# A fused retention and mixture-of-experts kernel: when weight chunks are loaded, when an early group is routed, and which banks the experts write to

## The chip, the cores and the metric

The kernel runs on one core of one Trainium2 chip. The metric is the device time of one execution in microseconds (us). TensorE is PE (matmuls) and PEld (its weight loads) in the rows, VectorE is DVE, ScalarE is ACT, GpSimd is POOL, and SP is the engine whose queue issues the plain DMAs.

## The reference

Eight batches of eight heads, 576 positions of 64 numbers each, go through a masked product without a softmax. The result is 4608 tokens of 512 numbers. Each token is sent to the one of eight experts whose embedding it is most like, and the expert's two-layer network is applied to it.

```python
scores = q @ k.T / sqrt(64)
x = (scores * gamma[h] ** (i - j) * (i >= j)) @ v          # per batch and head
x = x.transpose(0, 2, 1, 3).reshape(4608, 512)
logits = normalized(x) @ normalized(expert_emb).T / tau
e = argmax(logits); gate = softmax(logits)[e]
out = gate * (relu(x @ w1[e]) @ w2[e])                     # 512 -> 1024 -> 512, float32
```

## The kernel before

**The stream.** The 4608 tokens are 36 tiles of 128, and two batches are nine tiles, so the jobs around a tile repeat every nine tiles. Within this part (`manual_schedule`) every engine does its work in the order in which the code emits it. Iteration t of the loop does the following.

- It issues the loads of q/k and k/v of tile t+6 (`load_qk`, `load_kv`, seven buffers each).
- It emits the scores of the next tile, `emit_A(t + 1)`, into the two banks `pa`, and `emit_mask(t + 1)`, two VectorE products (L600) that read these banks. So the scores of tile t+2 cannot start before the mask of t+1 has read the banks.
- GpSimd scales the values of tile t+2 (`scale_v`, L583).
- `emit_QT`, `emit_O` and `emit_U` make the output of tile t in the two banks `po` and add to the running state in `pst`; `emit_X` (VectorE) takes the output from `po`.
- `emit_T(t - 1)` turns the previous tile by four matmuls against the identity (L134); ScalarE copies it (L689), SP stores it to `xd`.
- The jobs in the list `jobs[t]` come last: the steps of the routing, and the split of a weight chunk.

**Routing.** The tiles are eight groups of four or five. A group whose last tile is tl gets `route_logits` in iteration tl+1, `route_turn` and `route_head` in tl+2, `route_rank` and `route_onehot` in tl+3 (some ten VectorE steps, the last of them L308 to L323), `route_table` in tl+4. Group 6 (tiles 27 to 30) is the last that is routed inside the stream. Behind its table, in iteration 34, come `slots_to_tokens` and the first three gathers (`gather(0, i)`, an indirect DMA issued by GpSimd, L375), which fetch expert 0's first 384 tokens from `xd`. Behind the loop, `xprep(0, i)` turns what was gathered (L134, then L397 and L398), and the first layer of expert 0 starts.

**Weights.** Each weight matrix comes in four chunks of 128 x 1024 numbers. A chunk is loaded to a `raw` buffer (of seven), copied to a rounded part by ScalarE (L188), and VectorE makes the remainder (L189). Chunks of the first matrix are loaded and split in the jobs of iterations 12, 16, 20 and 24:

```python
wq = wsplit_tasks(0)
for i in range(4):
    at(12 + 4 * i, wq.pop(0))
```

**Experts.** This part is ordered by a planner, which moves instructions on each engine by its own estimates. For an expert e, `mm1` or `mm1_round` make the first layer, by 12 matmuls for each of eight blocks f and two token ranges, into the banks `pm` (range 0) and `pa`, `pst` (range 1), evicted by L805 and L806. `mm2(e, i)` makes the second layer for the i-th 128 tokens by 24 matmuls (L866); ScalarE multiplies by the gate (L873) and GpSimd scatters the rows (L874). `mm2` writes to two banks in turn, which are the halves of the stream's one tile `po`, except for i = 2, which has a `pm` bank:

```python
po = psp.tile([P, 2, 512], F32, name="po")
pso = Banks([po[:, 0, :], po[:, 1, :]])
```

The tokens of expert e+1 are gathered meanwhile (`gather`), turned by a transposing DMA (`xturn`, L413 and L414) and joined again (`xjoin`, L420, L397, L398).

Of the kernel before, what the change touches and what calls it, by code (L numbers as in the profile page):

```python
# [9 lines left out]
F32 = mybir.dt.float32  # L10
# [8 lines left out]
P = 128  # L19
B, H, S, D = 8, 8, 576, 64  # L20
# [8 lines left out]
NT = N // P  # L29
# [7 lines left out]
RW = 1032  # L37
# [56 lines left out]
def retention_moe(ctx: ExitStack, tc: tile.TileContext, qk, kv, embT, tau, w1, w2, cst, out):  # L94
# [6 lines left out]
    my = ctx.enter_context(tc.tile_pool(name="my", bufs=3))  # L101
    psp = ctx.enter_context(tc.tile_pool(name="psp", bufs=1, space=PSUM))
    pa = [psp.tile([P, 512], F32, name=f"pa{i}") for i in range(2)]
    po = psp.tile([P, 2, 512], F32, name="po")
    pst = psp.tile([P, 512], F32, name="pst")

    class Banks:
# [6 lines left out]
            return self.banks[(self.n - 1) % len(self.banks)]  # L114

    psa = Banks(pa + [pst])
    pso = Banks([po[:, 0, :], po[:, 1, :]])
    psm = Banks([psp.tile([P, 512], F32, name=f"pm{i}") for i in range(3)])

    def after(*ins):  # L120
# [48 lines left out]
    ss_all = keep.tile([P, NT], F32, name="ss_all")  # L169


    def wsplit_tasks(n):

        e, second = divmod(n, 2)
        src = (w2 if second else w1)[e]

        def step(c):
            raw = rawp.tile([P, RW], F32, name="raw")[:, :1024]
            if second:
                nc.sync.dma_start(  # L180
                    out=raw.rearrange("p (c n) -> p c n", c=2),
                    in_=src[c * 256 : (c + 1) * 256, :].rearrange("(c p) n -> p c n", p=P),
                )
            else:
                nc.sync.dma_start(out=raw, in_=src[c * P : (c + 1) * P, :])
            sl = wslot[n % 3]
            hi = sl[:, 0, c * 1024 : (c + 1) * 1024]
            nc.scalar.copy(hi, raw)  # L188
            nc.vector.tensor_tensor(  # L189
                out=sl[:, 1, c * 1024 : (c + 1) * 1024], in0=raw, in1=hi.bitcast(F32), op=ALU.subtract  # L190
            )

        return [lambda c=c: step(c) for c in range(4)]


    grp = {}
# [1 line left out]
    def group_tiles(b):  # L198
        t0 = (b // 2) * 9 + (0 if b % 2 == 0 else 4)
        return t0, (4 if b % 2 == 0 else 5)  # L200
# [170 lines left out]
    def gather(e, i, rows=N):  # L371
        a = _slot(e, i)
        t = rawp.tile([P, RW], F32, name="raw")
        xg[e, i] = t
        return nc.gpsimd.indirect_dma_start(  # L375
            out=t[:, :DM],
            out_offset=None,
            in_=xd[:rows, :],
            in_offset=bass.IndirectOffsetOnAxis(ap=gid[:, a : a + 1], axis=0),
        )  # L380
# [96 lines left out]
    with ExitStack() as att:  # L477
# [4 lines left out]
        a2 = att.enter_context(tc.tile_pool(name="a2", bufs=2))  # L482
        a1 = att.enter_context(tc.tile_pool(name="a1", bufs=1))

        qkt, kvt = {}, {}

        def load_qk(t):
# [241 lines left out]
        jobs = {}  # L729

        def at(t, f):
            jobs.setdefault(t, []).append(f)
# [4 lines left out]
        for b in range(B - 1):  # L737
            t0, G = group_tiles(b)
            tl = t0 + G - 1
            at(tl + 1, lambda b=b: route_logits(b))  # L740
            at(tl + 2, lambda b=b: (route_turn(b), route_head(b)))
            at(tl + 3, lambda b=b: (route_rank(b), route_onehot(b)))
            at(tl + 4, lambda b=b: route_table(b))
            if b == B - 2:
                at(tl + 4, lambda: slots_to_tokens(0, 3))
                for i in range(3):
                    at(tl + 4, lambda i=i: gather(0, i, group_tiles(B - 1)[0] * P))
                at(tl + 4, route_bump)
        wq = wsplit_tasks(0)
        for i in range(4):  # L750
            at(12 + 4 * i, wq.pop(0))

        emit_A(0)
        emit_mask(0)
        scale_v(0, nc.vector)
# [2 lines left out]
        for t in range(NT):  # L758
            if t + NLOAD - 1 < NT:
                load_qk(t + NLOAD - 1)  # L760
                load_kv(t + NLOAD - 1)
            if t + 1 < NT:
                emit_A(t + 1)
                emit_mask(t + 1)
            if t + 1 < KT:
                decay(t + 1)
            if t + 2 < NT:
                scale_v(t + 2, nc.gpsimd)
            if t % KT == 4:
                emit_O(t)  # L770
                emit_QT(t)
                emit_U(t)
            else:
                emit_QT(t)
                emit_O(t)
                emit_U(t)
            emit_X(t)
            if t > 0:
                emit_T(t - 1)
            for f in jobs.pop(t, ()):  # L780
                f()
        assert not jobs, jobs
        b = B - 1
# [9 lines left out]


    with ExitStack() as moe:
        mw = moe.enter_context(tc.tile_pool(name="mw", bufs=1, reuse_waits="tile"))
        hs = mw.tile([P, 2, NF, CAP], F32R, name="hs")
        late["xs1"] = mw.tile([P, 2, NP, C1], F32R, name="xs1")
# [166 lines left out]
    with tc.If(ntile > 0):  # L965
        with ExitStack() as ov:
# [57 lines left out]
            with tc.For_i(0, ntile, 1) as i:  # L1024
                ex = nc.sync.value_load(tei[0:1, bass.ds(i, 1)], min_val=0, max_val=NE - 1)
                w1s = op.tile([P, NP, FF], F32, name="w1s")
                nc.sync.dma_start(out=w1s, in_=w1[bass.ds(ex, 1)].rearrange("o (d p) n -> p (o d) n", p=P))
                w2s = op.tile([P, NF, DM], F32, name="w2s")
                nc.sync.dma_start(out=w2s, in_=w2[bass.ds(ex, 1)].rearrange("o (f p) n -> p (o f) n", p=P))
                ent = op.tile([P, 1], F32, name="ent")  # L1030
                nc.sync.dma_start(out=ent, in_=od[bass.ds(i * P, P), :])
                of = op.tile([P, 3], F32, name="of")
                nc.vector.tensor_scalar(
                    out=of[:, 0:1], in0=ent[:, 0:1], scalar1=-1.0, scalar2=0.0, op0=ALU.add, op1=ALU.max
                )
                nc.vector.tensor_scalar(
                    out=of[:, 2:3], in0=ent[:, 0:1], scalar1=0.0, scalar2=BIG, op0=ALU.is_equal, op1=ALU.mult
                )
                nc.vector.tensor_tensor(out=of[:, 1:2], in0=of[:, 0:1], in1=of[:, 2:3], op=ALU.add)
                oi = op.tile([P, 2], I32, name="oi")  # L1040
                nc.vector.tensor_copy(oi, of[:, :2])
                go = op.tile([P, 1], F32, name="go")
                nc.gpsimd.indirect_dma_start(
                    out=go,
                    out_offset=None,
                    in_=gd[:, :],
                    in_offset=bass.IndirectOffsetOnAxis(ap=oi[:, 0:1], axis=0),
                )
                xo = op.tile([P, DM], F32, name="xo")
                nc.gpsimd.indirect_dma_start(  # L1050
                    out=xo,
                    out_offset=None,
                    in_=xd[:, :],
                    in_offset=bass.IndirectOffsetOnAxis(ap=oi[:, 0:1], axis=0),
                )
                px = psm.tile([P, 512], F32, name="m")
                for d in range(NP):
                    nc.tensor.transpose(px[:, d * P : (d + 1) * P], xo[:, d * P : (d + 1) * P], ident)
                xTo = op.tile([P, NP, P], F32, name="xTo")
                nc.vector.tensor_copy(xTo, px.rearrange("p (r n) -> p r n", r=NP))  # L1060
                ho = op.tile([P, NF, P], F32, name="ho")
                for f4 in range(NF // 4):
                    ph = psm.tile([P, 512], F32, name="m")
                    for fi in range(4):
                        f = 4 * f4 + fi
                        for d in range(NP):
                            nc.tensor.matmul(
                                ph[:, fi * P : (fi + 1) * P],
                                w1s[:, d, f * P : (f + 1) * P],
                                xTo[:, d, :],  # L1070
                                start=(d == 0),
                                stop=(d == NP - 1),
                            )
                    nc.scalar.activation(
                        ho[:, 4 * f4 : 4 * f4 + 4, :], ph.rearrange("p (f n) -> p f n", f=4), AF.Relu
                    )
                py = pso.tile([P, 512], F32, name="o")
                for f in range(NF):
                    nc.tensor.matmul(py, ho[:, f, :], w2s[:, f, :], start=(f == 0), stop=(f == NF - 1))
                yo = op.tile([P, DM], F32, name="yo")  # L1080
                nc.scalar.activation(yo, py, AF.Copy, scale=go)
                nc.gpsimd.indirect_dma_start(
                    out=out[:, :],
                    out_offset=bass.IndirectOffsetOnAxis(ap=oi[:, 1:2], axis=0),
                    in_=yo,
                    in_offset=None,
                    bounds_check=N - 1,
                    oob_is_err=False,
                )
# [41 lines left out]
```

## Time and profile before

| | |
|---|---|
| median of 3 runs | 658.37 us (654.74 to 665.71) |
| profiled execution | 659.78 us, of it the profile's span 657.9 us |
| mean granted TensorE clock | 0.966 |
| PE busy | 606.0 us (92%) |
| DVE, ACT, POOL busy | 317.7, 222.7, 184.7 us |
| one tile's q/k, k/v, store | 512, 512, 256 KB |
| one weight chunk | 512 KB |

The rows that the prediction names come from this one execution; times in them count from the start of the span. A stretch's granted clock is 1.00 at 2.4 GHz and 0.50 at 1.2 GHz; values between are a mix of these two.

### The profile page before, as it was taken

The page shows a single profiled execution, that of the slowest core. Times are in us where ns is not written, and L with a number is a line of the kernel's source. Part 1 is how long each engine was busy: PE and PEld are TensorE (multiplying, and loading weights), DVE is VectorE, ACT ScalarE, POOL GpSimd, SP SyncE. Part 2 cuts the span into 40 slices and gives each one's busy share as a digit, 9 for nine tenths or more (in the row PEclk, how much of TensorE's full clock was granted, in tenths as well). Part 3 has the DMA queues.
Part 4 walks back from the last instruction along what each step waited for, and adds up shares of the span by engine and source line. Part 5 has one row for each costly group of instructions (what it writes and reads, how often), then busy time and mean ns, then how long its engine had stood idle before and what let it go on. Part 6 is the DMA issues. An engine that isn't in the chain of part 4 may idle for free.

```text
span 657.9 us, 12597 instructions
## 1 busy us (share of the span) xinstructions
PE 606.0 (92%) x5090; PEld 529.7 (81%) x5090; DVE 317.7 (48%) x626; ACT 222.7 (34%) x427; POOL 184.7 (28%) x179
## 2 busy tenths in 40 slices
PE   7999769769979898999999999998999999999985
PEld 7888658658859697988897898897899789889974
DVE  4576555466736657673266155337406615531200
ACT  1444333324443245433253243243315324332110
POOL 3842122111032544413151331324314033111011
PEclk8999789789979999999999999999999999999998
DMA  8999585677142829576149229519616832910010
GB/s 321 407 379 339 212 298 206 229 272 253 67 150 80 257 85 277 172 161 214 48 138 259 93 83 208 181 51 178 224 49 148 247 104 76 183 42 34 1 40 36
DMA packets 76323, 111.89 MB, mean 170 GB/s; under 512 B 44970, under 2 KB 45262, under 8 KB 76240
## 3 DMA queue, kind: packets, MB, share of 16 engines
q1 hardware_dynamic: 68560, 90.74, 45.0%
q0 software_dynamic: 7680, 19.95, 9.5%
q8 instruction: 63, 1.03, 0.6%
q14 instruction: 20, 0.16, 0.1%
HBM read 82.08 MB, written 19.94 MB: 155 GB/s over the span
## 4 chain that ended last, share of the span: by engine, by line
PE 71%; issue 12%; DMA 6%; DVE 6%; ACT 4%; POOL 1%; SPq 0%; POOLq 0%; DVEq 0%; ACTq 0%
PE po L866 20%; PE pa L130 15%; PE pm L130 14%; PE po L130 7%; PE pst L130 7%; PE pm L866 4%; PE pm L134 3%; DMA raw<-w 3%; DVE wslot L189 2%; ACT y L873 1%; ACT wslot L188 1%; DMA raw<-raw 1%; DMA qkt<-qk 1%; DVE pm L600 1%; POOL out L874 1%
## 5 line engine op out<-in xcount | busy, mean ns | idle before, releaser
L866 PE MATMUL po<-wslot,hs 128*128 128x512 f32 (+1 forms) x816 | 196.7, 391 | 16.8 <-ACT y L873 13.4
L866 PEld LDWEIGHTS po<-wslot,hs 128*128 128x128 f32 x816 | 147.6, 189 | 54.4 <-ACT y L873 21.2
L874 POOL DMA_INDIRECT out<-y,sid x40 | 43.1, 1076 | 260.7 <-ACT y L873 198.9
L130 PE MATMUL pm<-xs,wslot 128*128 128x320 f32 (+4 forms) x672 | 106.7, 314 | 0.9 <-DVE xs L398 0.7
L130 PEld LDWEIGHTS pm<-xs,wslot 128*128 128x128 f32 x672 | 103.0, 188 | 3.1 <-DVE xs L398 1.0
L189 DVE TENSOR_TENSOR wslot<-raw,wslot 128x1024 fp32r<-128x1024 f32 x64 | 77.7, 1219 | 41.8 <-ACT wslot L188 41.3
L873 ACT ACTIVATE y<-po,gt 128x512 f32<-128x512 f32 (+1 forms) x34 | 22.9, 674 | 184.5 <-issue 115.6
L130 PE MATMUL pa<-xs,wslot 128*128 128x256 f32 (+1 forms) x576 | 80.2, 290 | 0.1
L188 ACT CAST wslot<-raw 128x1024 fp32r<-128x1024 f32 x64 | 67.0, 1053 | 33.5 <-DMA raw<-w 29.5
L130 PEld LDWEIGHTS pa<-xs,wslot 128*128 128x128 f32 x576 | 76.3, 191 | 1.3 <-DVE xs L398 0.4
L130 PE MATMUL pa<-qkt 64*128 64x128 f32 x576 | 50.4, 308 | 21.3 <-DVE pm L600 18.3
L583 POOL TENSOR_TENSOR kvt<-kvt,cs 128x512 f32<-128x512 f32 x35 | 37.0, 1058 | 108.1 <-DMA kvt<-kv 105.3
L130 PEld LDWEIGHTS pa<-qkt 64*128 64x128 f32 x576 | 42.0, 206 | 29.6 <-DVE pm L600 20.6
L375 POOL DMA_INDIRECT raw<-xd,gid x40 | 40.7, 1017 | 72.2 <-DVE wslot L189 30.7
L806 DVE SCALAR_TENSOR_TENSOR hs<-pm,hs 128x384 fp32r<-128x384 f32 x56 | 29.9, 551 | 61.4 <-ACT hs L805 58.5
L600 DVE TENSOR_TENSOR pm<-pa,tri 128x512 f32<-128x512 f32 x64 | 41.1, 684 | 29.4 <-PE pa L130 29.4
L386 POOL DMA_INDIRECT gt<-gd,gid x40 | 45.7, 1142 | 12.2 <-issue 12.2
L806 DVE SCALAR_TENSOR_TENSOR hs<-pa,hs 128x256 fp32r<-128x256 f32 (+1 forms) x48 | 21.0, 437 | 56.3 <-ACT hs L805 54.7
L130 PE MATMUL po<-pm,kvt 128*64 128x128 f32 x576 | 43.1, 296 | 0.0
L130 PE MATMUL pst<-xs,wslot 128*128 128x256 f32 (+1 forms) x288 | 41.5, 288 | 0.8 <-issue 0.8
L663 ACT COPY T<-pst 128x256 f32<-128x256 f32 x32 | 11.9, 372 | 83.6 <-PE pst L130 83.6
L130 PEld LDWEIGHTS pst<-xs,wslot 128*128 128x128 f32 x288 | 38.6, 191 | 1.9 <-issue 1.2
(123 smaller groups left out, 595.7 us busy)
## 6 DMA issues: line engine op xcount, KB each, us to landing
raw<-w SPq DMA_DIRECT2D x64, 512.0 KB
qkt<-qk SPq DMA_DIRECT2D x36, 512.0 KB
kvt<-kv SPq DMA_DIRECT2D x36, 512.0 KB
xd<-y SPq DMA_DIRECT2D x36, 256.0 KB
raw<-xd,gid POOLq DMA_INDIRECT x40
gt<-gd,gid POOLq DMA_INDIRECT x40
out<-y,sid POOLq DMA_INDIRECT x40
raw<-raw SPq DMA_TRANSPOSE x37
```

The costliest lines, as they stand in the source:

```text
L130: pe[:] = [nc.tensor.matmul(*args, **kw)]
L134: pe[:] = [nc.tensor.transpose(*args, **kw)]
L188: nc.scalar.copy(hi, raw)
L189: nc.vector.tensor_tensor(out=sl[:, 1, c * 1024 : (c + 1) * 1024], in0=raw, in1=hi.bitcast(F32), op=ALU.subtract)
L375: return nc.gpsimd.indirect_dma_start(out=t[:, :DM], out_offset=None, in_=xd[:rows, :], in_offset=bass.IndirectOffsetOnAxis(ap=gid[:, a : ...
L386: nc.gpsimd.indirect_dma_start(out=g[:, i : i + 1], out_offset=None, in_=gd[:, :], in_offset=bass.IndirectOffsetOnAxis(ap=gid[:, a : a + 1 ...
L583: eng.tensor_tensor(out=v, in0=v, in1=gneg[:, t % KT].unsqueeze(2).broadcast_to([P, H, D]), op=ALU.mult)
L600: nc.vector.tensor_tensor(out=pm[:, h], in0=pa[h].rearrange("p (c n) -> p c n", c=NP), in1=m.unsqueeze(1).broadcast_to([P, NP, P]), op=ALU ...
L806: v = nc.vector.scalar_tensor_tensor(out=hs[:, 1, f, o : o + n], in0=ps[:, :n], scalar=0.0, in1=hi.bitcast(F32), op0=ALU.max, op1=ALU.subt ...
L866: nc.tensor.matmul(ps[:, :step], hs[:, hsp, f, i * P : (i + 1) * P], w[:, ws, f, n : n + step], start=(f == 0 and k == 0), stop=(f == NF - ...
L873: nc.scalar.activation(y[:, n : n + step], ps[:, :step], AF.Copy, scale=gts[e][:, i : i + 1])
L874: sc = nc.gpsimd.indirect_dma_start(out=out[:, :], out_offset=bass.IndirectOffsetOnAxis(ap=sid[:, a : a + 1], axis=0), in_=y, in_offset=No ...
```

## The change

1. Loading and splitting a chunk are two steps. The four chunks of the first matrix are loaded in the jobs of iterations 11, 15, 19 and 23 and split in those of 15, 19, 23 and 27.
2. Group 6 is routed a tile sooner: `route_logits` is taken ahead of `emit_T(30)` in iteration 31, and turn and head follow in the same iteration; rank and one-hot come in 32; table, slots, gathers and bump in 33.
3. In iteration 0 the scores and the mask of tile 1 are emitted behind `emit_X(0)` instead of ahead of `emit_O(0)`.
4. `po` belongs to a pool of the stream alone. The experts have a pool `pso` of two tiles of a bank each. The overflow path, which this data does not enter, writes to `psa`.

```diff
-    po = psp.tile([P, 2, 512], F32, name="po")
...
-    pso = Banks([po[:, 0, :], po[:, 1, :]])
...
-    def wsplit_tasks(n):
+    def wsplit_steps(n):
...
-        def step(c):
-            raw = rawp.tile([P, RW], F32, name="raw")[:, :1024]
+        raws = {}
+
+        def load(c):
+            raw = raws[c] = rawp.tile([P, RW], F32, name="raw")[:, :1024]
...
-            sl = wslot[n % 3]
+
+        def split(c):
+            raw, sl = raws.pop(c), wslot[n % 3]
...
-        return [lambda c=c: step(c) for c in range(4)]
+        return [(lambda c=c: load(c), lambda c=c: split(c)) for c in range(4)]
+
+    def wsplit_tasks(n):
+
+        return [lambda s=s: (s[0](), s[1]()) for s in wsplit_steps(n)]
...
+        pop = att.enter_context(tc.tile_pool(name="pop", bufs=1, space=PSUM))
+        po = pop.tile([P, 2, 512], F32, name="po")
...
+            soon = b == B - 2
             at(tl + 1, lambda b=b: route_logits(b))
-            at(tl + 2, lambda b=b: (route_turn(b), route_head(b)))
-            at(tl + 3, lambda b=b: (route_rank(b), route_onehot(b)))
-            at(tl + 4, lambda b=b: route_table(b))
-            if b == B - 2:
-                at(tl + 4, lambda: slots_to_tokens(0, 3))
+            at(tl + 1 + (not soon), lambda b=b: (route_turn(b), route_head(b)))
+            at(tl + 2 + (not soon), lambda b=b: (route_rank(b), route_onehot(b)))
+            at(tl + 3 + (not soon), lambda b=b: route_table(b))
+            if soon:
+                at(tl + 3, lambda: slots_to_tokens(0, 3))
                 for i in range(3):
-                    at(tl + 4, lambda i=i: gather(0, i, group_tiles(B - 1)[0] * P))
-                at(tl + 4, route_bump)
-        wq = wsplit_tasks(0)
-        for i in range(4):
-            at(12 + 4 * i, wq.pop(0))
+                    at(tl + 3, lambda i=i: gather(0, i, group_tiles(B - 1)[0] * P))
+                at(tl + 3, route_bump)
+        for i, (load, split) in enumerate(wsplit_steps(0)):
+            at(11 + 4 * i, load)
+            at(15 + 4 * i, split)
+
+        LATE = group_tiles(B - 1)[0]
...
-            if t + 1 < NT:
+            if 0 < t < NT - 1:
                 emit_A(t + 1)
                 emit_mask(t + 1)
...
             emit_X(t)
+            if t == 0:
+                emit_A(1)
+                emit_mask(1)
+            todo = jobs.pop(t, [])
+            if t == LATE:
+                todo.pop(0)()
             if t > 0:
                 emit_T(t - 1)
-            for f in jobs.pop(t, ()):
+            for f in todo:
                 f()
...
+        pso = moe.enter_context(tc.tile_pool(name="pso", bufs=2, space=PSUM, reuse_waits="tile"))
...
-                py = pso.tile([P, 512], F32, name="o")
+                py = psa.tile([P, 512], F32, name="o")
```

## Rows read from the trace of the kernel before

**Rows 1.** Stretches: start:end length, busy time by engine, PEclk, DMA share, GB/s.

```profile
25.45:62.40 36.95, 36.85 (x634) 30.77 (x633) 25.64 (x62) 15.97 (x39) 16.61 (x20) 1.00 1.00 371
62.40:166.22 103.82, 85.28 (x1268) 71.44 (x1267) 58.56 (x134) 35.20 (x81) 19.48 (x19) 0.87 0.68 245
62.40:71.40 9.00, 5.10 (x78) 3.47 (x76) 3.16 (x6) 4.13 (x9) 1.51 (x2) 0.93 0.75 278
71.40:78.49 7.09, 7.09 (x72) 6.21 (x72) 3.12 (x5) 0.78 (x3) 2.09 (x2) 0.61 0.48 175
184.00:197.25 13.25, 8.89 (x63) 5.94 (x60) 3.49 (x11) 5.26 (x13) 6.37 (x4) 0.74 0.55 177
224.00:652.00 428.00, 411.78 (x2376) 366.47 (x2376) 183.44 (x288) 143.04 (x252) 116.18 (x108) 1.00 0.48 131
```

**Rows 2.** Timeline around the first weight chunk: start, length, engine, line [idle before <-releaser].

```profile
61.66 1.28 DVE L600 TENSOR_TENSOR pm<-pa,trix 128x512 f32<-128x512 f32 x2
62.40 1.75 PE L130 MATMUL pa<-qkt 64*128 64x128 f32 x16
...
63.29 0.57 SPq L185 DMA_DIRECT2D raw<-w  x1
...
68.44 1.04 ACT L188 CAST wslot<-raw 128x1024 fp32r<-128x1024 f32 x1 [4.80 <-DMA raw<-w]
...
69.52 1.23 DVE L189 TENSOR_TENSOR wslot<-raw,wslot 128x1024 fp32r<-128x1024 f32 x1 [5.84 <-ACT wslot L188]
...
71.40 2.67 PE L130 MATMUL pa<-qkt 64*128 64x128 f32 x16 [3.79 <-DVE pm L600]
```

**Rows 3.** Timeline from the first gather to the first layer of expert 0.

```profile
184.32 1.19 POOL L375 DMA_INDIRECT raw<-xd,gid  x1 [17.84 <-DVE t L364]
...
188.01 0.63 PE L134 MATMUL pm<-ident,raw 128*128 128x128 f32 x4 [2.32 <-DMA raw<-xd,gid]
...
190.57 1.09 PE L134 MATMUL pm<-ident,raw 128*128 128x128 f32 x4 [1.93 <-DMA raw<-xd,gid]
...
197.25 4.26 PE L130 MATMUL pa<-xs,wslot 128*128 128x384 f32 x23
```

**Rows 4.** Waits of PE from 224 to 652: total, times, longest.

```profile
PE po L866 <- ACT y L873: 13.4, 16, 1.6
```

**Rows 5.** The scaling of values on GpSimd (tile kvt) up to 62.4 us.

```profile
L583 POOL TENSOR_TENSOR kvt<-kvt,cs x17: 1037/1047/1049, 10.8 to 61.8; 128x512 f32<-128x512 f32 x17
```

**Rows 6.** Timeline: one VectorE line twice, and GpSimd beside its second instance.

```profile
61.16 0.58 DVE L323 TENSOR_TENSOR rp<-ra,entry 128x400 bf16<-128x400 f32 x1
...
84.05 1.24 POOL L583 TENSOR_TENSOR kvt<-kvt,cs 128x512 f32<-128x512 f32 x1 [7.30 <-DMA kvt<-kv]
...
84.42 1.22 DVE L323 TENSOR_TENSOR rp<-ra,entry 128x320 bf16<-128x320 f32 x1
```

**Rows 7.** Timeline in the last expert's second layer.

```profile
630.69 0.69 ACT L873 ACTIVATE y<-po,gt 128x512 f32<-128x512 f32 x1 [5.13 <-PE po L866]
631.43 5.31 PEld L866 LDWEIGHTS po<-wslot,hs 128*128 128x128 f32 x24 [1.25 <-ACT y L873]
631.43 5.73 PE L866 MATMUL po<-wslot,hs 128*128 128x512 f32 x24 [0.83 <-ACT y L873]
...
637.25 0.69 ACT L873 ACTIVATE y<-po,gt 128x512 f32<-128x512 f32 x1 [5.87 <-PE po L866]
...
637.99 5.73 PE L866 MATMUL po<-wslot,hs 128*128 128x512 f32 x24 [0.83 <-ACT y L873]
```

**Rows 8.** Waits of PE from 250 to 300.

```profile
PE po L866 <- ACT y L873: 1.6, 1, 1.6
PE pm L130 <- DVE xs L398: 0.7, 1, 0.7
```

**Rows 9.** Chain of work that ended last: start, length, what.

```profile
244.96 7.17 DMA raw<-raw
...
257.83 3.95 PE pm L130 x23
```

**Rows 10.** Waits of PE from 622 to 652, the last expert's second layer.

```profile
PE po L866 <- ACT y L873: 3.1, 4, 0.8
```

**Rows 11.** Timeline at the start of the stream.

```profile
9.06 2.08 PE L130 MATMUL pa<-qkt 64*128 64x128 f32 x16 [2.71 <-DMA qkt<-qk]
13.05 1.16 PE L130 MATMUL pa<-qkt 64*128 64x128 f32 x16
```

## The prediction

> **What bounds the kernel now.** TensorE is busy for 606.0 of 657.9 us, so the page's table says only that time is gained where PE idles or runs slowly. I read the stretches first, cut where the jobs of the stream repeat. Nine tiles from 25.45 to 62.40, iterations 4 to 12, take 36.95 us, 4.1 each, with PE busy throughout and a granted clock of 1.00. The next eighteen, iterations 13 to 30, have the same routing jobs twice and take 103.82 us, with a clock of 0.87 and 18.5 us of idle PE [rows 1]. What the second stretch has and the first has not is the four weight chunks.
>
> The timeline shows why. A chunk's load is issued at 63.29, ScalarE sits until 68.44 for it, VectorE's remainder starts at 69.52, and behind that, in the same queue, stands the mask that frees the score banks. PE gets on at 71.40 after 3.79 us of idle [rows 2]. That stretch lasts 9.00 us, and the next 7.09 at a clock of 0.61, though PE is then busy all the time [rows 1]. So a chunk costs twice, in idle and in the slow matmuls behind it.
>
> Next I looked at the joint to the experts. From 184.00 to 197.25 PE is busy 8.89 of 13.25 us at a clock of 0.74 [rows 1]; it waits 2.32 and 1.93 us for gathered tokens [rows 3]. In the experts, 224 to 652, it is busy for 411.78 of 428.00 us at a clock of 1.00. Of the 16.2 idle, 13.4 are 16 waits of the second layer for ScalarE's eviction [rows 1, 4].
>
> **Chunks loaded ahead.** *Removed:* without stalls eighteen tiles take 2 x 36.95 = 73.9 us, so 103.82 - 73.90 = 29.9 us are the chunks' whole price, slow clock included. *Moved:* the load goes four tiles, 16 us, ahead of its use; it took about 5.1 us from 63.29 to 68.44 [rows 2]. On SP's queue it stands behind the store of the same iteration and ahead of the loads for tile t+7, which are six tiles early. GpSimd has scaled 17 tiles' values by 62.4, all but the first (VectorE's), so tile 17 has landed as iteration 13 starts, where tile 14 was due [rows 5]. Three tiles of cover hide the half microsecond of issue and the 512 KB.
>
> *Is there bandwidth?* Nine tiles need 9 x 1.25 MiB = 11.8 MB, and 2.25 chunks 1.2 MB more: 13.0 MB in some 39.4 us, 330 GB/s. The stretch without stalls moved 371 [rows 1], so the load fits.
>
> *Added:* the split stays. ScalarE's 1.04 us has room (15.97 of 36.95 us busy [rows 1]). VectorE's 1.23 us has not everywhere. In the tile behind rank and one-hot the mask ends at 62.94, while PE's next scores started at 62.40 and are stretched to 1.75 us [rows 2]; the slack is gone there already. The split of iteration 15 stands just behind a rank. Those of 19, 23 and 27 stand one or two tiles ahead of one, and push VectorE's queue into it. I bound a split by 0 (the slack takes it) and by 1.04 + 1.23 = 2.3 us (nothing of copy and remainder is hidden), and take VectorE's 1.23, nearest to the row of the crowded tile: 4 x 1.23 = 4.9 us. Gain 29.9 - 4.9 = **25.0**, ends 20.7 to 29.9.
>
> A neighbour could make it dearer. VectorE's L323 took 0.58 us at 61.16 and 1.22 at 84.42, on a smaller tile, with GpSimd's scaling (1.24 us) started just before it [rows 6]; the remainder, too, reads two SBUF operands, and a scaling takes 1.05 [rows 5]. If each of the four is held for a whole scaling, that is 4.2 us more. The Trainium skill (SBUF — State Buffer, Who interferes with whom) says a VectorE instruction with two SBUF inputs contends with a GpSimd one that reads SBUF, and that the later of the two is blocked until the earlier ends; the two lengths of L323 agree. By that rule the sum would be 4.2 worse at most; by the rows of the chunk in the stall, which had VectorE alone, it would be nothing.
>
> **Group 6 a tile sooner.** Logits, turn, head, rank, table, three gathers and bump are the same instructions; iteration 31 gets two steps, and 34, the last but one, loses its table. GpSimd's queue has no scaling left behind the gathers. The gathers read what tiles up to 30 stored; SP has issued the last of these stores in iteration 31, two tiles earlier, with no load behind it. They start about 4.1 us earlier, more than the 2.32 us of the first wait; the second, landing about 190.5, then lands at 186.4, near the time PE comes to it. Turn now waits in iteration 31 for the copy of its logits: some tenths. The joint loses 13.25 - 8.89 = 4.4 us of idle. At a mean of 0.74 about half the stretch ran at 1.2 GHz, 13.25 x 0.52 = 6.9 us, which at 2.4 GHz is 3.4 less: together 7.8, the upper end. The eviction of the last tokens (L397, L398) ahead of 197.25 stays late next, and I leave 1.7 us for it and the second gather: **6.1**, lower end 3.0 if the clock stays low and only the first wait and some tenths go.
>
> **Banks of their own.** Two halves of `po` should let the second layer write one while the other is evicted. The rows say otherwise: the matmuls at 637.99 start as the eviction that began at 637.25 ends, and that is the previous output, in the other half; their own was evicted from 630.69 on [rows 7]. The tile, not the bank, is what is waited for. With separate tiles a group waits for the eviction before the last, some 5.7 us old. Of the 13.4 us I leave out the wait of 1.6: it lies between experts 0 and 1, where PE next waits 0.7 us for the turned tokens, so that time would be given back there [rows 8], and the chain also goes through that transposing DMA [rows 9]. **11.8** is left. Lower end 3.1, the last expert's four waits, where there is no other work to plan around [rows 10]; upper end 16.2, all idle [rows 1]. The planner orders this part anew, so the pieces of next expert's first layer that fill gaps now will lie elsewhere.
>
> **The first tile.** Scores of tile 1 move behind the output of tile 0. They now wait 2.71 us for data; but tile 2's scores at 13.05 need tile 1's mask to have read the banks, and this mask gets later. I take 0, between -1 and +1 [rows 11].
>
> **The rivals.** *(a) Banks bring nothing:* each wait becomes one for `hs`, tokens or weights, since the planner already puts other matmuls in many gaps. 616.9 + 11.8 = 628.7. For it: PE is at 96% there. Against: the four waits at the end have nothing else to wait for. The Trainium skill (TensorE: Matmul & The Clock Gate, HAM oscillation — how this bites in real kernels) has a kernel where "Adding PSUM double-buffering gave no further gain"; by that the sum would be this case, while the 13.4 us of waits on evictions speak against it. Chance 0.12.
>
> *(b) The clock falls again at the splits:* VectorE's delay lets PE idle so long that the tile behind runs as from 71.40 on, 7.09 instead of 4.2 us [rows 1]; 4 x 2.9 = 11.6, to 628.5. Idle of 0.83 us in the experts left the clock at 1.00 [rows 1, 7], 3.79 did not [rows 2]; I expect 1.2. Chance 0.10.
>
> *(c) The split is locked out by GpSimd,* as weighed above: 616.9 + 4.2 = 621.1. Chance 0.08.
>
> *(d) The change does not do what it says in the stream:* faster tiles drain the transfer queue, so that a chunk or a tile lands late after all. If the chunks' 5.1 us of landing come back four times: 616.9 + 20.6 = 637. The 371 against 330 GB/s speak against it. Chance 0.05.
>
> *(e) Slower:* the planner closes up the second layer's groups, and the next expert's first layer stands behind its turned tokens, not beside other work. The transposes took 7.17 us on the chain once [rows 9]; bare at each of seven passages between experts they are 50.2, to 667. It decides when over 43/7 = 6.1 us of each are bare. Now PE waits for tokens 0.7 us in all [rows 8]. Chance 0.02.
>
> **How the numbers follow.** The profiled execution took 659.78 us, 1.9 over its span and 1.4 over the median of runs, which scatter over 11 us. 659.8 - 25.0 - 6.1 - 11.8 - 0 = 616.9 by that execution, 615.5 by the median; I say 616. The forecast has a chance of 0.63. All upper ends together give 659.8 - 29.9 - 7.8 - 16.2 - 1 = 604.9, all lower ends 659.8 - 20.7 - 3.0 - 3.1 + 1 = 634. The range 605 to 631 holds (a), (b) and (c) as well and leaves out (d) and (e). A difference of 2%, 13 us, is about what a measurement of this kernel can tell from none, so 645 is the border: only (e), and the far end of (d) with (a), pass it. Faster 0.95, same 0.03, slower 0.02.
>
> **What would show it.** In the profile after: no wait of ScalarE for a weight chunk in the stream; iterations 13 to 30 in about 79 us at a clock near 1.00, with the tile behind a split about a microsecond longer than its like; no wait over a microsecond for gathered tokens, and the joint's clock over 0.9; waits of the second layer on ScalarE near zero, and PE idle under 5 us in the experts. Wrong would be: masks late by more than 2 us, a chunk's copy still released by its DMA, or as much idle in the experts with another releaser.

## The result

The changed kernel takes 601.62 us (median of 4 runs, 600.11 to 603.70), the kernel before 656.89 in the same comparison; the ratio is 0.917, 95% interval [0.912, 0.922]. The sign was right. The time lies 3.4 us below the lower end of the forecast's range: the change brought more than all upper ends together allowed. The profiled execution of the changed kernel took 600.45 us, its span is 598.6 and its mean granted clock 0.997; set against the profiled execution of before, the span is 59.3 us shorter.

I cut both traces at the same work: at the start of the scores of tile 14 (iteration 13 begins) and of tile 32 (iteration 31), at the first long group of expert 0's first layer, at its second layer, and at the start of expert 1's first layer. The stretches of the profile after answer to [rows 1]; the columns are the same.

```profile
24.52:61.52 37.00, 36.88 (x633) 30.75 (x632) 25.54 (x62) 15.93 (x39) 16.99 (x20) 1.00 0.98 380
61.52:138.60 77.08, 75.50 (x1269) 62.60 (x1267) 55.92 (x133) 35.47 (x81) 18.10 (x17) 1.00 0.93 330
138.60:164.32 25.72, 24.25 (x371) 18.80 (x369) 16.50 (x46) 13.33 (x31) 6.38 (x5) 1.00 0.35 119
164.32:181.80 17.48, 17.48 (x108) 16.95 (x108) 12.29 (x43) 5.65 (x10) 5.89 (x3) 1.00 0.32 102
181.80:224.60 42.80, 42.79 (x241) 37.77 (x240) 30.14 (x61) 19.62 (x30) 23.09 (x20) 1.00 0.81 222
224.60:592.12 367.52, 365.81 (x2160) 332.77 (x2160) 163.12 (x252) 128.53 (x227) 101.87 (x95) 1.00 0.48 134
```

The same view of the kernel before, for the stretches that [rows 1] do not have:

```profile
166.22:197.25 31.03, 26.16 (x371) 20.31 (x370) 16.28 (x46) 13.56 (x31) 6.63 (x5) 0.89 0.33 111
197.25:214.66 17.41, 17.41 (x107) 16.83 (x108) 12.33 (x43) 5.65 (x10) 4.85 (x3) 1.00 0.25 80
214.66:264.97 50.31, 45.10 (x243) 37.68 (x243) 32.25 (x64) 20.38 (x31) 25.41 (x21) 1.00 0.74 216
264.97:651.42 386.45, 373.24 (x2160) 332.99 (x2159) 160.02 (x249) 126.11 (x225) 97.97 (x93) 1.00 0.46 124
```

| stretch | before | after | gained | forecast |
|---|---|---|---|---|
| up to iteration 13 | 62.40 | 61.52 | 0.9 | 0 |
| iterations 13 to 30 | 103.82 | 77.08 | 26.7 | 25.0 |
| joint, to expert 0's first layer | 31.03 | 25.72 | 5.3 | 6.1 |
| expert 0, first layer | 17.41 | 17.48 | -0.1 | |
| expert 0, the rest | 50.31 | 42.80 | 7.5 | |
| experts 1 to 7 | 386.45 | 367.52 | 18.9 | 11.8 for all experts |

From PE's last matmul to the end it is 6.5 us in both. So the banks brought 26.4 us (7.5 + 18.9) where 11.8 were forecast and 16.2 were held to be the most; the other terms together, 32.9 measured, are 1.8 over their forecast of 31.1.

**The stream.** The stretch of iterations 13 to 30 moved 330 GB/s at a clock of 1.00; before it moved 245 at 0.87. ScalarE no longer waits for a chunk in it. The timeline answers to [rows 2]: the split of the first chunk, all four engines.

```profile
75.55 1.03 ACT L189 CAST wslot<-raw 128x1024 fp32r<-128x1024 f32 x1
76.97 1.22 DVE L190 TENSOR_TENSOR wslot<-raw,wslot 128x1024 fp32r<-128x1024 f32 x1
77.89 1.20 POOL L591 TENSOR_TENSOR kvt<-kvt,cs 128x512 f32<-128x512 f32 x1 [3.15 <-DMA kvt<-kv]
78.10 1.28 DVE L608 TENSOR_TENSOR pm<-pa,tri 128x512 f32<-128x512 f32 x2
78.84 1.43 PE L128 MATMUL pa<-qkt 64*128 64x128 f32 x12 [0.56 <-DVE pm L608]
```

The copy begins with no wait in front of it. The remainder still stands ahead of the mask in VectorE's queue and PE waits 0.56 us for that mask, in place of 3.79.

**The joint.** The timeline answers to [rows 3]:

```profile
153.76 1.19 POOL L380 DMA_INDIRECT raw<-xd,gid  x1 [13.92 <-DVE t L369]
158.26 0.60 PE L132 MATMUL pm<-ident,raw 128*128 128x128 f32 x4
159.40 0.63 PE L132 MATMUL pm<-ident,raw 128*128 128x128 f32 x4 [0.54 <-DMA raw<-xd,gid]
164.32 4.28 PE L128 MATMUL pa<-xs,wslot 128*128 128x384 f32 x23
```

The first gather starts 10.6 us ahead of the first layer (12.9 before), yet the waits for gathered tokens are down from 4.25 us to 0.54, since PE has tile work while they land; the clock stays at 1.00.

**The experts.** What PE waits for from 224.6 to 592.12 answers to [rows 4]; then the same of its weight loads. Waits whose releaser the profile does not name (0.2 us of PE, 0.8 of the weight loads) are left out.

```profile
PE pa L128 <- ACT xs L402: 0.5, 1, 0.5
PE o L883 <- ACT y L890: 0.4, 1, 0.4
PE pa L128 <- DVE xs L403: 0.3, 1, 0.3
```

```profile
PEld pa L128 <- ACT xs L402: 1.1, 2, 0.8
PEld pa L128 <- DVE xs L403: 0.8, 2, 0.5
PEld o L883 <- ACT y L890: 0.8, 1, 0.8
```

One wait for an eviction is left. Those for turned and rejoined tokens, named in rival (e), came to 0.8 us in PE's rows, not to 43.

### The profile page after: what moved, and what is told of

It is laid out like the page before. It is cut to its first block, busy times and chain, and to the rows that moved or that the text cites. A ratio compares the mean times of both kernels' runs of the same rounds, so it can differ in the third digit from the quotient of the medians.

```text
span 598.6 us, 12604 instructions
## 1 busy us (share of the span) xinstructions
PE 583.3 (97%) x5090; PEld 517.8 (87%) x5090; DVE 316.5 (53%) x626; ACT 224.4 (37%) x427; POOL 186.2 (31%) x179
## 5 line engine op out<-in xcount | busy, mean ns | idle before, releaser
L883 PE MATMUL o<-wslot,hs 128*128 128x512 f32 (+1 forms) x816 | 186.6, 384 | 0.5 <-ACT y L890 0.4
L883 PEld LDWEIGHTS o<-wslot,hs 128*128 128x128 f32 x816 | 148.6, 188 | 29.5 <-ACT y L890 0.8
L380 POOL DMA_INDIRECT raw<-xd,gid x40 | 42.0, 1051 | 74.2 <-DVE wslot L190 34.1
L890 ACT ACTIVATE y<-o,gt 128x512 f32<-128x512 f32 (+1 forms) x34 | 22.6, 674 | 107.0 <-PE o L883 92.1
L128 PE MATMUL pa<-qkt 64*128 64x128 f32 x576 | 45.8, 286 | 2.7 <-DVE pm L608 1.9
L128 PEld LDWEIGHTS pa<-qkt 64*128 64x128 f32 x576 | 37.4, 187 | 10.6 <-DVE pm L608 4.9
L822 ACT ACTIVATE hs<-pa 128x256 fp32r<-128x256 f32 (+1 forms) x48 | 19.2, 399 | 68.2 <-PE pa L128 59.4
L128 PE MATMUL po<-pm,kvt 128*64 128x128 f32 x576 | 39.4, 279 | 2.0 <-DVE kvt L591 2.0
```

Of the source, the lines that this page charges most:

```text
L128: pe[:] = [nc.tensor.matmul(*args, **kw)]
L380: return nc.gpsimd.indirect_dma_start(out=t[:, :DM], out_offset=None, in_=xd[:rows, :], in_offset=bass.IndirectOffsetOnAxis(ap=gid[:, a : ...
L822: a = nc.scalar.activation(hi, ps[:, :n], AF.Relu)
L883: nc.tensor.matmul(ps[:, :step], hs[:, hsp, f, i * P : (i + 1) * P], w[:, ws, f, n : n + step], start=(f == 0 and k == 0), stop=(f == NF - ...
L890: nc.scalar.activation(y[:, n : n + step], ps[:, :step], AF.Copy, scale=gts[e][:, i : i + 1])
```

## The experiments

Each kernel is the one before or the changed one with the edit shown, and each ratio, with its 95% interval, is to the kernel before, whose median beside these runs was 658.8 to 660.1 us. Lines left out of an edit are marked by `...`. "Stretch 13 to 30", "joint" and "experts" (from expert 0's first layer to PE's last matmul: 454.17 before, 427.80 after) are read as above.

**Banks alone**, the kernel before with part 4 only:

```diff
-    po = psp.tile([P, 2, 512], F32, name="po")
...
-    pso = Banks([po[:, 0, :], po[:, 1, :]])
...
+        pop = att.enter_context(tc.tile_pool(name="pop", bufs=1, space=PSUM))
+        po = pop.tile([P, 2, 512], F32, name="po")
...
+        pso = moe.enter_context(tc.tile_pool(name="pso", bufs=2, space=PSUM, reuse_waits="tile"))
...
```

> Part 4 alone on the kernel before (the experts' second layer gets a pool of two tiles, the stream keeps its own po). Theory 1: the shared tile alone cost what the experts gained after the change, 7.5 us in expert 0 and 18.9 behind it, 26.4 in all whatever the stream does: about 630.5 us, ratio 0.96. Rival, theory 2: the banks are worth the 11.8 us of the forecast, and the rest comes because the faster stream hands over on better terms (weights and tokens landed earlier): about 645 us, ratio 0.98.

Measured: 632.81 us, ratio 0.959 [0.955, 0.964]. The stretch 13 to 30 is 104.04 as before, the experts take 428.24: 25.9 us, by this part alone. That is theory 1; the interval leaves out theory 2's 0.98.

**Two halves of one tile again**, the changed kernel with an own tile for the experts that holds both banks:

```diff
-        pso = moe.enter_context(tc.tile_pool(name="pso", bufs=2, space=PSUM, reuse_waits="tile"))
+        pos = moe.enter_context(tc.tile_pool(name="pos", bufs=1, space=PSUM, reuse_waits="tile"))
+        po2 = pos.tile([P, 2, 512], F32, name="po2")
+        pso = Banks([po2[:, 0, :], po2[:, 1, :]])
```

> The changed kernel, but the experts' two outputs are again the halves of one tile, now a tile of a pool of the experts' own. Theory 1: what counts is that two outputs share a tile, so all of the 26.4 us come back: about 628 us, and the weight loads of the second layer wait some 20 us for the eviction. Rival, theory 3: the pool that opens behind the stream frees the planner, and sharing a tile matters little: about 602 to 614 us.

Measured: 629.58 us, 0.953 [0.947, 0.958]; experts 455.56, about the 454.17 of before. The waits of the weight loads from 224 to 640 are near the 20 us expected:

```profile
PEld po L885 <- ACT y L892: 22.2, 23, 3.2
```

**One bank only**:

```diff
-        pso = moe.enter_context(tc.tile_pool(name="pso", bufs=2, space=PSUM, reuse_waits="tile"))
+        pso = moe.enter_context(tc.tile_pool(name="pso", bufs=1, space=PSUM, reuse_waits="tile"))
```

> The changed kernel with one buffer in place of two in the experts' pool, so each second-layer output must wait for the eviction of the one before it. Theory 1: two halves of a shared tile behave as one bank, so this is as slow as the halves: 626 to 630 us. Rival (the halves do overlap in part, and only the planner is misled): clearly slower than the halves, 635 us or more.

Measured: 629.25 us, 0.956 [0.950, 0.961]; experts 453.12. PE's waits for an eviction from 224 to 640, and then those of its weight loads:

```profile
PE o L883 <- ACT y L890: 11.8, 15, 0.8
```

```profile
PEld o L883 <- ACT y L890: 19.0, 22, 1.3
```

Two banks in one tile and a single bank cost the same, and as much as the kernel before. So in this kernel the second bank was worth nothing as long as it was the other half of a tile.

**Expert 0 on one bank**, the others on two:

```diff
-        pso = moe.enter_context(tc.tile_pool(name="pso", bufs=2, space=PSUM, reuse_waits="tile"))
+        pos = moe.enter_context(tc.tile_pool(name="pos", bufs=1, space=PSUM, reuse_waits="tile"))
+        o01 = [pos.tile([P, 512], F32, name=f"o{i}") for i in range(2)]
+        pso = Banks(o01)
...
-                ps = wide[2] if part else pso.tile([P, 512], F32, name="o")
+                ps = wide[2] if part else (pso.tile([P, 512], F32, name="o") if e else o01[0])
```

> The changed kernel with two fixed one-bank tiles, of which expert 0 uses only the first; the others take both in turn. If the 7.5 us of expert 0 came because two outputs can be open at once while the last weight chunk is still being split: they come back, about 609 us. If they came from an earlier landing of the chunks or another order of the planner: 601 to 603 us.

Measured: 612.82 us, 0.930 [0.925, 0.935]; experts 435.26, 7.5 more than the changed kernel. The whole is 4 us over the 609 expected: the joint is 2.0 longer in this trace and tile 14 starts 2.7 later, two places that vary as much between runs without this edit. The stretches, cut as above, show where the 7.5 lie:

```profile
168.47:185.96 17.49, 17.49 (x107) 16.96 (x108) 12.30 (x43) 5.65 (x10) 5.89 (x3) 1.00 0.32 101
185.96:236.26 50.30, 45.53 (x245) 37.98 (x245) 32.12 (x64) 20.54 (x32) 25.66 (x21) 1.00 0.75 219
236.26:603.73 367.47, 365.04 (x2158) 331.93 (x2156) 161.24 (x249) 128.12 (x225) 100.78 (x93) 1.00 0.47 130
```

Expert 0's rest is back at the 50.3 of before, experts 1 to 7 stay at the 367.5 of after. Since these tiles are fixed and not dealt out by a pool, the pool isn't the cause either.

**Chunks alone**, the kernel before with part 1 only (its two functions and these lines):

```diff
-        wq = wsplit_tasks(0)
-        for i in range(4):
-            at(12 + 4 * i, wq.pop(0))
+        for i, (load, split) in enumerate(wsplit_steps(0)):
+            at(11 + 4 * i, load)
+            at(15 + 4 * i, split)
```

> Part 1 alone on the kernel before (chunks loaded four tiles ahead of their splits). Forecast: 25.0 us less; by the trace after, iterations 13 to 30 take 26.7 us less: 630 us, ratio 0.96. Theory 2 (the stream's gain carries on into the experts): about 615 to 620 us.

Measured: 635.12 us, 0.965 [0.958, 0.971]; the stretch 13 to 30 takes 77.62, 26.2 less, and the experts 454.81. The whole is 5 us over the 630 expected, and further from theory 2's 615 to 620; nothing carries on into the experts.

**Loaded in the iteration of the split**, the changed kernel without the lead:

```diff
-            at(11 + 4 * i, load)
+            at(15 + 4 * i, load)
```

> The changed kernel, but each chunk is loaded in the iteration of its split (15, 19, 23, 27), so that only the place of the splits is new. If the four tiles of lead are what took the stall away: the 26.7 us come back, 626 to 630 us. If it was the place (other tiles, faster landing): under 610 us.

Measured: 633.26 us, 0.960 [0.955, 0.965], a little over the first expectation and far from the second. The stretch takes 104.95 at a clock of 0.87, and the stall is back in ScalarE's waits from 60 to 170:

```profile
ACT wslot L189 <- DMA raw<-w: 22.1, 4, 6.3
```

**A lead of one iteration**:

```diff
-            at(11 + 4 * i, load)
+            at(14 + 4 * i, load)
```

> The changed kernel with a chunk loaded one iteration ahead of its split (jobs of 14, 18, 22, 26; splits stay in 15, 19, 23, 27). Theory: what counts is that the load's landing is over when ScalarE's queue comes to the copy; landing took 5.1 us from issue in the kernel before, an iteration takes 4.1, so each chunk can stall ScalarE for about 1 us and iterations 13 to 30 take 77 to 81 us; the whole is 602 to 606 us. Rival: with the other loads in the queue a landing takes far longer than 5 us when the tiles come fast, so that the four iterations of lead are needed; then iterations 13 to 30 take over 85 us and the whole over 610.

Measured: 607.29 us, 0.920 [0.915, 0.925]; the stretch takes 82.47, 5.4 more than with four iterations of lead. Both expectations missed it: over the one's 81, well under the other's 85. ScalarE's waits from 60 to 140:

```profile
ACT wslot L189 <- DMA raw<-w: 4.2, 3, 1.8
```

One iteration hides 21.3 of the 26.7 us. Three of the four chunks are late by up to 1.8 us: issued at 74.32, 90.75 and 129.08, they are copied at 79.63, 97.84 and 134.87, that is 5.3, 7.1 and 5.8 us later, where an iteration has 4.1.

**Splits moved off the crowded tiles**, the changed kernel with

```diff
-            at(11 + 4 * i, load)
-            at(15 + 4 * i, split)
+            at((13, 14, 22, 23)[i], load)
+            at((17, 18, 26, 27)[i], split)
```

> The changed kernel with the splits in iterations 17, 18, 26 and 27, whose neighbours give VectorE little to do, and the loads four tiles ahead as before. By the trace after, the splits behind 15, 19 and 23 still stretch iterations by 3.1 us in all and the one of 27 by nothing. If VectorE's crowded tiles are the cause: about 3 us less than the changed kernel, 598 to 599 us. If the price is the split's own 1.2 us wherever it stands: no change, 601 to 602 us.

Measured: 604.67 us, 0.915 [0.911, 0.920], above both expectations. The intervals overlap with the changed kernel's: no measurable difference. The stretch is 76.14, where five traces with the splits in 15, 19, 23 and 27 have 76.44 to 78.06; iterations 19, 27 and 28 are stretched now, by 0.2 to 0.6 us, and the joint is 29.11. So the 3 us do not come back by moving the splits, and crowded tiles are not shown to be the cause; what sets the price of a split stays open.

**Group 6 sooner, alone**, the kernel before with part 2 only:

```diff
+            soon = b == B - 2
             at(tl + 1, lambda b=b: route_logits(b))
...
+            at(tl + 1 + (not soon), lambda b=b: (route_turn(b), route_head(b)))
...
```

> Part 2 alone on the kernel before (group 6 routed a tile sooner). Forecast 6.1 us less; the trace after shows 5.3 between tile 32's scores and the first layer: 651 to 654 us, too little for one comparison of runs, to be read from the trace: no wait over 1 us for gathered tokens, and the clock of the joint near 1.00.

Measured: 658.03 us, 0.996 [0.993, 0.999] over 10 runs, above the 651 to 654 expected; the joint takes 27.61, 3.4 less, at a clock of 1.00 and with no wait for gathered tokens. But PE waits for something new in it, ScalarE's copy of the running state for the last tile:

```profile
186.68 0.67 PE L130 MATMUL po<-qkt,T 64*64 64x128 f32 x16 [2.40 <-ACT T L663]
```

Of the eight traces with this part four have this wait, 2.4 us each time (this one, the loads in the iteration of the split, expert 0 on one bank, the splits moved), and joints of 27.6 to 29.1 us; the other four, the changed kernel among them, do not, and have 25.5 to 25.8. None of the four traces without this part has it; their joints take 29.95 to 31.03. What holds ScalarE there is not shown.

**The first tile alone**, the kernel before with part 3 only:

```diff
-            if t + 1 < NT:
+            if 0 < t < NT - 1:
                 emit_A(t + 1)
...
             emit_X(t)
+            if t == 0:
+                emit_A(1)
+                emit_mask(1)
```

> The kernel before with part 3 alone (scores and mask of tile 1 behind the output of tile 0). Theory, as predicted: nothing measurable, scores of tile 14 start within 1 us of 62.4, ratio 0.995 to 1.005. Rival: the start of 0.9 us that the changed kernel gained (61.52) is this part's, and tile 14 starts at 61.5 here as well.

Measured: 660.93 us, 1.002 [0.999, 1.005] over 12 runs; tile 14 starts at 62.12. In four traces without this part it starts between 61.06 and 62.64, in eight with it between 61.52 and 64.31 (means 62.2 and 63.0): the 0.9 us of the table lies within the scatter.

The four ratios of the parts alone multiply to 0.959 x 0.965 x 0.996 x 1.002 = 0.924, near the 0.917 of all: that they help or hurt each other is not measurable, to about 1%.

## Why the prediction was right or wrong

**Banks of their own: right mechanism, mis-sized.** This is the step that failed: "11.8 is left", and with it "upper end 16.2, all idle"; the term measured 26.4 us, 25.9 by this part alone. That the tile and not the bank is waited for was right, as the runs with two halves and with one bank show. The size was wrong for two reasons.

First, I read it from the waits in PE's matmul rows, whose ends are modelled, and the modelled end covers part of a hole. In [rows 7] two groups of 24 matmuls start at 631.43 and 637.99, 6.56 us apart. Without a hole 24 take 5.45: after, 72 take 16.52 and 48 take 11.07 us, so the 24 more take 5.45. The hole is 6.56 - 5.45 = 1.11 us. PE's row draws the group 5.73 long and says 0.83; PEld's says 1.25. For experts 1 to 7 the waits of the kernel before are, in the two views:

```profile
PE po L866 <- ACT y L873: 11.8, 15, 0.8
PE po L866 <- DVE hs L806: 1.3, 1, 1.3
```

```profile
PEld po L866 <- ACT y L873: 19.0, 22, 1.3
PEld po L866 <- DVE hs L806: 2.5, 3, 1.7
```

22 waits instead of 15, 19.0 us instead of 11.8; 18.9 were gained. So idle time was no ceiling: of those 18.9, PE's idle gave 11.5 (13.21 to 1.71) and its "busy" 7.4 (373.24 to 365.81, for the same 2160 matmuls).

Second, expert 0. My stretch of the experts began at 224, behind the first holes of its second layer, and their releasers do not name the banks. Before, in PE's timeline:

```profile
214.66 3.34 PE L866 MATMUL po<-wslot,hs 128*128 128x512 f32 x13
219.22 1.66 PE L866 MATMUL po<-wslot,hs 128*128 128x512 f32 x6 [1.22 <-issue]
221.67 1.41 PE L866 MATMUL po<-wslot,hs 128*128 128x512 f32 x5 [0.79 <-DVE wslot L189]
223.85 0.39 PE L130 MATMUL pst<-xs,wslot 128*128 128x256 f32 x1 [0.77 <-issue]
...
247.01 5.63 PE L866 MATMUL po<-wslot,hs 128*128 128x512 f32 x24
254.26 2.60 PE L866 MATMUL po<-wslot,hs 128*128 128x512 f32 x10 [1.62 <-ACT y L873]
```

and after, in PE's, then in ScalarE's:

```profile
181.80 16.52 PE L883 MATMUL o<-wslot,hs 128*128 128x512 f32 x72
...
209.67 11.07 PE L883 MATMUL o<-wslot,hs 128*128 128x512 f32 x48
```

```profile
189.97 0.69 ACT L890 ACTIVATE y<-o,gt 128x512 f32<-128x512 f32 x1 [0.21 <-PE o L883]
192.97 0.69 ACT L890 ACTIVATE y<-o,gt 128x512 f32<-128x512 f32 x1 [1.80 <-issue]
198.36 0.69 ACT L890 ACTIVATE y<-o,gt 128x512 f32<-128x512 f32 x1 [4.70 <-PE o L883]
```

The last chunks of the second matrix are split while this layer runs, equally late in both kernels. VectorE's remainder of the last chunk starts 5.2 us behind the layer's first matmul, before and after:

```profile
219.84 1.22 DVE L189 TENSOR_TENSOR wslot<-raw,wslot 128x1024 fp32r<-128x1024 f32 x1
```

```profile
187.01 1.22 DVE L190 TENSOR_TENSOR wslot<-raw,wslot 128x1024 fp32r<-128x1024 f32 x1
```

Before, one output could be open, and PE stood still twice in it. After, 72 matmuls run without a hole, and the first two evictions come 3.0 us apart where one output alone needs 5.45: the second output was begun while the first still lacked its last chunk. With one bank for expert 0 the whole 7.5 us went. Late weights are a third to a half of it. By starts, the first group took 9.19 us to the next matmul (214.66 to 223.85) where 24 take 5.45: the two holes cost 2.7 us, the wait behind the group, whose releaser is not named, 1.0. The group at 247.01 took 7.25 to the next, 1.8 for the eviction; 1.0 was the wait for turned tokens [rows 8], which after falls into the next stretch; the rest is in smaller pieces. The experiment took all of it back at once and does not divide it. I had called the waits I left out, 1.6 us between experts 0 and 1, time that would be given back; it was not.

**Chunks loaded ahead: right.** 26.7 measured (26.2 alone) for 25.0, within its ends of 20.7 and 29.9. Load in the iteration of the split and all of it returns, slow clock included. The splits cost 77.08 - 2 x 37.00 = 3.1 us, not 4.9 (2.4 to 4.1 over the five traces with these splits): that of iteration 27 stretched no tile. The bandwidth that the step worked out, 330 GB/s, is what the stretch moved.

**Group 6 a tile sooner: right mechanism, size not settled.** 5.3 for 6.1: idle of PE fell from 4.87 to 1.47 us, and with the clock at 1.00 its busy time from 26.16 to 24.25. The gathers started 2.9 us earlier, counted from tile 32's scores, not 4.1. The 5.3 is from a trace without the wait for ScalarE's copy; alone, with this wait, the part gave 3.4, near the lower end. The mean joints of the eight traces with the part and of the four without differ by 3.7 us. The sum had no term for that wait.

**The first tile: right,** nothing.

**The rivals.** (a) *Banks bring nothing:* no, 26 us. The case weighed there, from the Trainium skill (TensorE: Matmul & The Clock Gate, HAM oscillation — how this bites in real kernels), is of a kernel in which a second PSUM buffer gave no further gain; it doesn't carry over to this one. With one bank the experts take 453.12 us here, with two 427.80. (b) *The clock falls at the splits:* no; it is 1.00 over the stretch, where PE waits for masks three times, 1.1 us in all and 0.6 at most. (c) *Locked out:* did not decide. The four remainders took 1.22 to 1.23 us in the changed kernel; in none of them was a scaling running when it started. It does happen, as the last section shows. (d) and (e): no.

## What to carry to other kernels

Where several matmuls wait for an eviction, take the size from the weight-load rows or from the distance of starts against that of a dense group, and don't treat PE's idle time as a ceiling. Two PSUM banks that are halves of one tile may be waited for as one: look whether a group starts at the end of its neighbour's eviction. A second output that can be opened is also work for PE while weights are late, so look for such waits under the name of the weights, too.

## What the runs showed of the hardware

**VectorE and GpSimd in each other's way.** In the run with two halves a scaling on GpSimd, 1.05 us where nothing is in its way [rows 5], began just behind a remainder on VectorE:

```profile
80.00 1.99 POOL L591 TENSOR_TENSOR kvt<-kvt,cs 128x512 f32<-128x512 f32 x1 [2.36 <-DMA kvt<-kv]
```

```profile
79.87 1.22 DVE L190 TENSOR_TENSOR wslot<-raw,wslot 128x1024 fp32r<-128x1024 f32 x1
```

They overlap for 1.09 us, and the later took 0.94 longer. In the changed kernel, as shown for the first chunk, an overlap of 0.30 us cost the scaling 0.15. In the run with the splits moved it was the remainder that came later, at 124.19 into a scaling that ran from 123.59 to 124.64: 0.45 us of overlap, and it took 1.53 in place of 1.22. Each time the earlier kept its length, and the later lost the overlap less about 0.15 us. That agrees with the Trainium skill (SBUF — State Buffer, Who interferes with whom), by which the later one is blocked until the earlier ends, to within that 0.15.

**Landing of a chunk.** In the run with a lead of one iteration the three chunks that ScalarE waited for took 5.3, 7.1 and 5.8 us from issue to copy. In the kernel before the four took 4.2 to 5.5, and in the run with the loads in the iteration of the split 5.0 to 7.3. So the 5.1 of one chunk [rows 2] is not an upper bound. What makes the longer ones longer was not tested.
